# Regrouped wo rows and two reordered steps in a one-token attention and feed-forward kernel

## The chip, the cores and the metric

The kernel runs on 1 core of one Trainium2 chip. The metric is the device time of one execution in microseconds. Below, PE is TensorE, DVE is VectorE, ACT is ScalarE, and SP is the engine that issues nearly all DMAs here.

## What is computed

One token `x` (512 values, bf16) passes through attention over a cache of 65536 keys and values in 32 heads of 128, and beside it through a small feed-forward block; a scalar gate mixes the two.

```python
# H, Sk, Dh = 32, 65536, 128;  D = 512;  F = 1792
q = (x @ wq).reshape(H, Dh)
scores = einsum("hd,hkd->hk", q, k_cache) * Dh ** -0.5
o = einsum("hk,hkd->hd", softmax(scores), v_cache)
a = o.reshape(H * Dh) @ wo                    # wo: 4096 x 512
b = (silu(x @ w_gate) * (x @ w_up)) @ w_down
g = sigmoid((x * gate_w).sum())
out = g * a + (1 - g) * b
```

The two caches are 512 MB each, 1073.7 MB of the 1087.6 MB that are read. Keys and values are read once.

## The kernel before

**Tiling.** A head's 65536 keys are cut into 4 blocks of 128 x 128 keys; there are N = 128 blocks, numbered n = 4h + g, and M = 64 pairs of blocks, numbered i. A key block lies in SBUF as 128 partitions x 128 keys x 128 dimensions.

**Buffers.** Two slots take a pair of key blocks each (8 MB; `take` and `give`). `V_buf` takes a pair of value blocks; before that it holds wq, then w_gate, w_up and w_down. At the very end the two key slots are used again: `wo_early` holds wo of heads 0 to 15 and V block 124, `wo_late` holds V block 127 and wo of heads 16 to 31.

**Steps for a block n.** `products(n)` (DVE, L252 and L256) multiplies the keys with the broadcast q and halves the width by adding until 32 columns are left. `scores(n)` (PE, L265) adds these up with an identity as weights into PSUM; after it the key slot is free. `fold(n)` (DVE, L280) reduces the last four columns into `S_sb`. `values(n)` (PE, L321) multiplies the probabilities with the value block, 32 matmuls of 4 keys a partition each, into `O_ps`; after it that half of `V_buf` is free. For the very last block 30 matmuls do so, and 8 small ones (L339) the rest.

**Steps for a head h.** `query(h)` broadcasts q over the partitions (L166, L168, L170). `row_max(h)` and `exponentials(h)` find the maximum (a transpose on PE, L290) and make the probabilities (ACT, L299). `total(h)` adds the exponentials (PE, L307), `weight(h)` makes the factor gate / total, `rg` (DVE). `head_copy(h)` brings `O_ps` to SBUF (ACT, L331), `head_turn(h)` turns it into a column by 4 matmuls (L347) and writes that column, times `rg`, to `oT[:, h]` (ACT, L354). `project(h)` multiplies `oT[:, h]` with wo's 128 rows of head h into two accumulators (PE, L360).

**Loads.** `load_k`, `load_v` (L111) and `load_wo` (L176) are all issued from SP's queue in program order; each load waits there until its buffer is free, and what stands behind it waits as well. V blocks 125, 126 and 127 come in 2, 2 and 6 pieces (`V_CUTS`), wo's second half in 4 (`LATE_CUTS`). `load_wo` copies runs of one row of wo, 512 values, 1 KB: partition p gets row 128h + p for each head h.

**Order.** The order on each engine is that of the program, written out by hand; a loop over the 64 pairs interleaves the steps, so that values are two pairs behind the scores. In pair i PE does values(2i - 4), scores(2i) and values(2i - 3) and then scores(2i + 1); where a head starts (`first`), scores(2i) comes ahead of the values. w_down's product (`feed_forward_mid` on DVE, `feed_forward_out` on PE) comes in pair 1, after the first DVE step of products(3) and fold(2); behind it V block 0 is loaded, into the buffer that w_down leaves. In the last pair the projections of the first 16 heads stand ahead of scores(127). After the loop come head 31's softmax, head 30's turn, the last four values, head 31's turn and the projections of heads 16 to 31.

Of the kernel before, what the change touches and what calls it, by code (L numbers as in the profile page):

```python
# [8 lines left out]
ACT = mybir.ActivationFunctionType  # L9
ALU = mybir.AluOpType  # L10
AXIS = mybir.AxisListType
P = 128
# [7 lines left out]
QUAD = 4  # L20
# [3 lines left out]
TURNED = 8  # L24
V_CUTS = {3: (0, 64, NB), 2: (0, 64, NB), 1: (0, 32, 64, 96, 112, NB - TURNED, NB)}
EARLY = 16
LATE_CUTS = (EARLY, 21, 26, 30, 32)


@with_exitstack  # L30
def kernel(
# [14 lines left out]
    nc = tc.nc  # L46
# [11 lines left out]
    M = N // 2  # L58
    MH = G // 2
    assert Dh == P and G == 4 and NBH == 512 and H * D <= PAIR * Dh  # L60
    scale = float(Dh) ** -0.5
# [32 lines left out]
    with nc.allow_non_contiguous_dma(reason="small"):  # L94
# [4 lines left out]
        out=V_buf[:, : KT * H * Dh], in_=A_wq.rearrange("(p t) f -> p (t f)", t=KT)  # L99
# [3 lines left out]
    K_tiles, V_tiles, S_tiles, F_tiles, P_tiles, O_tiles, q_tiles = {}, {}, {}, {}, {}, {}, {}  # L103


    def load(view, cache, m, cuts, start=0):
        h, g = divmod(m, MH)
        rows = cache[0, h, g * PAIR * P : (g + 1) * PAIR * P, :]
        src = rows.rearrange("(p j) d -> p j d", j=PAIR)
        for a, b in zip(cuts[:-1], cuts[1:]):  # L110
            nc.sync.dma_start(out=view[:, a:b, :], in_=src[:, start + a : start + b, :])  # L111
# [7 lines left out]
    def load_v(n, half=0, spare=None):  # L119
        if n % G == 0 and spare is None:  # L120
            view = V_buf.rearrange("p (j d) -> p j d", d=Dh)
            V_tiles[n], V_tiles[n + 1] = view[:, :NB, :], view[:, NB:, :]
            load(view, A_v_cache, n // 2, (0, PAIR))
        else:
            view = V_buf if spare is None else spare
            view = view[:, half * NB * Dh : (half + 1) * NB * Dh]
            V_tiles[n] = view = view.rearrange("p (j d) -> p j d", d=Dh)
            load(view, A_v_cache, n // 2, V_CUTS.get(N - n, (0, NB)), n % 2 * NB)
# [16 lines left out]
    oT = consts.tile([P, H], bf16, name="oT")  # L145
    gval = consts.tile([P, 1], f32, name="gval")
    rg = consts.tile([P, H], f32, name="rg")
# [23 lines left out]

    def load_wo(tile, cuts):
        t = tile[:, : H * D].rearrange("p (h n) -> p h n", n=D)
        rows = A_wo.rearrange("(h p) n -> p h n", p=P)
        for a, b in zip(cuts[:-1], cuts[1:]):
            nc.sync.dma_start(out=t[:, a:b, :], in_=rows[:, a:b, :])  # L176
        return t

    def feed_forward_in():
# [63 lines left out]
    def width_of(n):  # L243
        return FIRST if n < G else WIDTH

    def products(n):
        K = K_tiles[n]
        qb = q_tiles[n // G][:, :]
        q_rep = bass.AP(
            tensor=qb.tensor, offset=qb.offset, ap=[list(qb.ap[0]), [0, NB], [1, Dh]]  # L250
        )
        yield nc.vector.tensor_tensor(out=K, in0=K, in1=q_rep, op=ALU.mult)  # L252
        half = Dh
        while half > width_of(n):
            half //= 2
            yield nc.vector.tensor_tensor(  # L256
                out=K[:, :, 0:half], in0=K[:, :, 0:half], in1=K[:, :, half : 2 * half],
                op=ALU.add,
            )

    def scores(n):
        S = F_tiles[n] = psum_s.tile([P, NB, QUAD], f32, name="S_ps")
        width = width_of(n)
        for c in range(0, width, QUAD):
            nc.tensor.matmul(  # L265
                S,
                lhsT=ident_b,
                rhs=K_tiles[n][:, :, c : c + QUAD],
                start=(c == 0),
                stop=(c == width - QUAD),  # L270
            )
        del K_tiles[n]
        if n % 2:
            give(f"K_t.{n // 2}")

    def fold(n):
        h, g = divmod(n, G)
        if g == 0:
            S_tiles[h] = small.tile([P, NBH], f32, name="S_sb")
        nc.vector.tensor_reduce(  # L280
            out=S_tiles[h][:, g * NB : (g + 1) * NB], in_=F_tiles.pop(n), axis=AXIS.X, op=ALU.add
        )
# [10 lines left out]
    def exponentials(h, mT_ps):  # L293
        top = small.tile([P, 1], f32, name="top")
        nc.vector.tensor_reduce(out=top, in_=mT_ps, axis=AXIS.X, op=ALU.max)  # L295
        bias = small.tile([P, 1], f32, name="bias")
        nc.scalar.activation(out=bias, in_=top, func=ACT.Copy, scale=-scale)  # L297
        P_tiles[h] = small.tile([P, NBH], bf16, name="P_sb")
        nc.scalar.activation(  # L299
            out=P_tiles[h], in_=S_tiles[h], func=ACT.Exp, bias=bias, scale=scale,  # L300
            accum_out=rowsum[:, h : h + 1],
        )
        del S_tiles[h]

    def total(h):
        tot_ps = psum_m.tile([P, 1], f32, name="tot_ps", tag="misc")
        nc.tensor.matmul(tot_ps, lhsT=ones_f, rhs=rowsum[:, h : h + 1], start=True, stop=True)  # L307
        return tot_ps
# [19 lines left out]

    def head_copy(h):
        O_sb = small.tile([4, 4 * Dh], f32, name="O_sb", tag="row", bufs=1)  # L330
        nc.scalar.activation(out=O_sb, in_=O_tiles.pop(h), func=ACT.Copy)  # L331
        return O_sb

    def head_turn(h, O_sb):
        oh_ps = psum_m.tile([P, 1], f32, name="oh_ps", tag="misc")
        turned = range(NB - TURNED, NB) if h == H - 1 else ()
        for j in turned:
            k = (G - 1) * NB + j
            nc.tensor.matmul(  # L339
                oh_ps,  # L340
                lhsT=V_tiles[N - 1][:, j, :],
                rhs=P_tiles[h][:, k : k + 1],
                start=(j == turned[0]),
                stop=False,
            )
        for c in range(4):
            nc.tensor.matmul(  # L347
                oh_ps,
                lhsT=O_sb[:, c * Dh : (c + 1) * Dh],
                rhs=ident_f[0:4, c : c + 1],  # L350
                start=(c == 0 and not turned),
                stop=(c == 3),
            )
        nc.scalar.activation(  # L354
            out=oT[:, h : h + 1], in_=oh_ps, func=ACT.Copy, scale=rg[:, h : h + 1]
        )

    def project(h):
        for i, a in enumerate(a_ps):
            nc.tensor.matmul(  # L360
                a,
                lhsT=oT[:, h : h + 1],
                rhs=wo_sb[:, h, i * HD : (i + 1) * HD],
                start=False,
                stop=(h == H - 1),
            )
# [11 lines left out]
    for i in range(M):  # L378
        h, first = i // MH, i % MH == 0
        vector = products(2 * i)  # L380
        next(vector)
        if mT_ps is not None:
            exponentials(h - 1, mT_ps)
        if not first:
            fold(2 * i - 1)
        for _ in vector:
            pass
        if first:
            scores(2 * i)
        if i >= 2:  # L390
            values(2 * i - 4)
            if first or i == M - 1:
                load_v(2 * i - 2 if first else N - 3)
        if not first:
            scores(2 * i)
        if i == 0:
            xs = gate_sum()
            eg2 = gate_exp(xs)
        if i >= 2:
            values(2 * i - 3)  # L400
            if first or i == M - 1:
                load_v(2 * i - 1 if first else N - 2, 1)
            else:
                load_v(2 * i - 2)
        if mT_ps is not None:
            tot_ps = total(h - 1)
            mT_ps = None
        if first and i > MH:
            head_turn(h - 2, head_copy(h - 2))
        vector = products(2 * i + 1)  # L410
        next(vector)
        fold(2 * i)
        if i == 1:
            hT = feed_forward_mid(*ff)
            feed_forward_out(hT, rest)
            load_v(0)
        for _ in vector:
            pass
        if i == 0:
            rest = gate_value(eg2)  # L420
        if tot_ps is not None:
            weight(h - 1, tot_ps)
            tot_ps = None
        if not first and h + 1 < H:
            query(h + 1)
        if i == M - 1:
            for o in range(EARLY):
                project(o)
        scores(2 * i + 1)
        if i == 0:  # L430
            ff = feed_forward_in()
        if i + 2 < M:
            load_k(i + 2)
        elif i + 2 == M:
            spare = take("wo_early.0")
            wo_sb = load_wo(spare, (0, EARLY))
            load_v(N - 4, 1, spare)
        if not first:
            fold(2 * i + 1)
            mT_ps = row_max(h)  # L440
    spare = take("wo_late.0")
    load_v(N - 1, 1, spare)
    exponentials(H - 1, mT_ps)
    tot_ps = total(H - 1)
    head_turn(H - 2, head_copy(H - 2))
    values(N - 4)
    values(N - 3)
    weight(H - 1, tot_ps)
    wo_sb = load_wo(spare, LATE_CUTS)
    values(N - 2)  # L450
# [39 lines left out]
```

## Time and profile before

| | |
|---|---|
| Median of 3 runs | 2529.11 us (2528.47 to 2530.81) |
| Profiled execution, its own time | 2529.75 us |
| Its span | 2528.0 us |
| Mean granted TensorE clock | 0.759 |
| Busy in the span: PE, DVE, ACT | 1415.6, 2065.9, 90.8 us |
| DMA | 1088.48 MB in 29577 packets, mean 431 GB/s |

The span is the time from the first to the last instruction of one profiled execution; its own time is the device time of that same execution. Busy times are sums over an engine's instructions. A row of the timeline gives start, duration, engine, line, operation and, in brackets, how long the engine was idle before it and what ended that. A row that merges several instructions has "xN" at its end. For SP's queue a merged row holds the time between the issues too. Matmul ends are modelled, so neighbouring PE rows can overlap by a fraction of a microsecond.

### The profile page before, as it was taken

Reading aid. Unit: us, or ns where it says so; the run is one execution under the profiler, and the core shown is the slowest. Engines: PE = TensorE matmul, PEld = TensorE weight load, DVE = VectorE, ACT = ScalarE, POOL = GpSimd, SP = SyncE. Lnnn points to the kernel's source line nnn. Section 1 sums busy time; section 2 is a strip of 40 time slices with the busy share of each in tenths; the row PEclk is TensorE's granted clock in tenths of the full one; section 3 lists DMA queues with packets and bytes.
Section 4 is the critical chain, followed back from the end, with each engine's and each line's share of the span. In section 5 each row is a group of like instructions: output and inputs, shape, how many; then the busy total and the mean of one; then the engine's idle time right before and its main releaser. Section 6 shows DMA issues by size and latency. Waiting matters only on the chain.

```text
span 2528.0 us, 13114 instructions
## 1 busy us (share of the span) xinstructions
PE 1415.6 (56%) x5898; PEld 548.2 (22%) x5898; DVE 2065.9 (82%) x648; ACT 90.8 (4%) x264; POOL 0.7 (0%) x6
## 2 busy tenths in 40 slices
PE   3655654646646456555465464665555655646648
PEld 2212221212212122222122121221212221212214
DVE  5897888887878878879888888788797888887882
ACT  0000000000000000000000000000000000000000
POOL 0000000000000000000000000000000000000000
PEclk9777777778777677777777776776867877768769
DMA  9999999999999999999999999999999999999998
GB/s 415 428 440 432 433 432 433 437 433 432 435 430 433 439 436 433 432 429 435 437 434 433 430 433 435 437 432 430 434 438 432 435 434 428 435 436 432 432 431 341
DMA packets 29577, 1088.48 MB, mean 431 GB/s; under 512 B 3153, under 2 KB 7250, under 8 KB 7634
## 3 DMA queue, kind: packets, MB, share of 16 engines
q1 hardware_dynamic: 29234, 1087.65, 99.6%
q8 instruction: 46, 0.75, 0.1%
q14 instruction: 9, 0.07, 0.0%
q10 hardware_dynamic: 288, 0.00, 0.0%
HBM read 1087.64 MB, written 0.00 MB: 430 GB/s over the span
## 4 chain that ended last, share of the span: by engine, by line
DMA 62%; PE 33%; DVE 4%; issue 0%; ACT 0%; another core or an unknown queue 0%; SPq 0%; DVEq 0%; ACTq 0%
DMA V_buf<-in_A_v_cache_dram 56%; PE O_ps L321 29%; DMA K_t<-in_A_k_cache_dram 6%; PE S_ps L265 3%; DVE K_t L252 3%; DVE K_t L256 1%; PE a_ps L360 0%; PE oh_ps L347 0%; PE b_ps L233 0%; DVE S_sb L280 0%; DVE top L295 0%; ACT O_sb L331 0%; PE a_ps L239 0%; PE qb_ps L168 0%
## 5 line engine op out<-in xcount | busy, mean ns | idle before, releaser
L252 DVE TENSOR_TENSOR K_t<-K_t,q_sb 128x16384 bf16<-128x16384 bf16 x128 | 1112.0, 8687 | 216.9 <-DMA K_t<-in_A_k_cache_dram 216.9
L321 PE MATMUL O_ps<-V_buf,P_sb 128*4 128x512 bf16 x4032 | 960.0, 401 | 363.0 <-DMA V_buf<-in_A_v_cache_dram 361.5
L256 DVE TENSOR_TENSOR K_t<-K_t 128x8192 bf16<-128x8192 bf16 x252 | 849.1, 3369 | 4.3
L265 PE MATMUL S_ps<-K_t,ident_b 128*128 128x512 bf16 x1056 | 352.9, 492 | 662.4 <-DVE K_t L256 662.4
L321 PEld LDWEIGHTS <-P_sb 128*4 128x4 bf16 x4094 | 359.3, 88 | 986.1 <-issue 524.2
L265 PEld LDWEIGHTS <-ident_b 128*128 128x128 bf16 x1056 | 116.1, 115 | 844.1 <-issue 759.6
L280 DVE TENSOR_REDUCE S_sb<-S_ps 128x128 f32<-128x512 f32 x128 | 87.6, 685 | 118.5 <-PE S_ps L265 118.5
L312 DVE RECIPROCAL recip<-tot_ps 128x1 f32<-128x1 f32 x32 | 5.4, 168 | 79.4 <-PE tot_ps L307 79.4
L290 PE MATMUL mT_ps<-diag,ones_f 128*128 128x128 f32 x64 | 21.5, 430 | 62.0 <-ACT diag L288 62.0
L170 ACT ACTIVATE q_sb<-qb_ps 128x128 bf16<-128x128 f32 x32 | 8.9, 277 | 955.2 <-PE qb_ps L168 955.2
L354 ACT ACTIVATE oT<-oh_ps,rg 128x1 bf16<-128x1 f32 x32 | 8.4, 264 | 736.6 <-PE oh_ps L347 736.6
L347 PE MATMUL oh_ps<-ident_f,O_sb 4*128 4x1 f32 x256 | 34.3, 251 | 0.5 <-ACT O_sb L331 0.5
L290 PEld LDWEIGHTS mT_ps<-diag,ones_f 128*128 128x128 f32 x64 | 13.4, 261 | 89.4 <-ACT diag L288 89.4
L347 PEld LDWEIGHTS oh_ps<-ident_f,O_sb 4*128 4x128 f32 x256 | 31.6, 190 | 1.2 <-ACT O_sb L331 0.7
L457 DVE CAST out_sb<-a_ps 1x256 bf16<-1x256 f32 x1 | 0.4, 411 | 36.6 <-PE a_ps L360 36.6
L288 ACT ACTIVATE diag<-ident_f,m 128x128 f32<-128x128 f32 x32 | 12.8, 401 | 303.0 <-DVE m L286 303.0
L299 ACT ACTIVATE P_sb<-S_sb,bias 128x512 bf16<-128x512 f32 x32 | 23.1, 722 | 1.0
L286 DVE TENSOR_REDUCE m<-S_sb 128x1 f32<-128x512 f32 x32 | 21.9, 686 | 1.1
L331 ACT ACTIVATE O_sb<-O_ps 4x512 f32<-4x512 f32 x32 | 18.2, 570 | 29.5 <-PE O_ps L321 29.5
L297 ACT ACTIVATE bias<-top 128x1 f32<-128x1 f32 x32 | 6.5, 203 | 327.2 <-DVE top L295 327.2
L307 PE MATMUL tot_ps<-rowsum,ones_f 128*128 128x1 f32 x64 | 12.2, 261 | 1.5 <-ACT P_sb L299 1.5
L307 PEld LDWEIGHTS tot_ps<-rowsum,ones_f 128*128 128x128 f32 x64 | 9.5, 188 | 15.2 <-issue 13.5
(48 smaller groups left out, 108.8 us busy)
## 6 DMA issues: line engine op xcount, KB each, us to landing
V_buf<-in_A_v_cache_dram SPq DMA_DIRECT2D x62, 4096.0 KB, 23.0
K_t<-in_A_k_cache_dram SPq DMA_DIRECT2D x4, 4096.0 KB, 32.5
V_buf<-in_A_v_cache_dram SPq DMA_DIRECT2D x4, 2048.0 KB, 25.0
V_buf<-in_A_wq_dram SPq DMA_DIRECT2D x1, 4096.0 KB, 12.5
wo_early<-in_A_v_cache_dram SPq DMA_DIRECT2D x1, 4096.0 KB, 35.4
wo_late<-in_A_v_cache_dram SPq DMA_DIRECT2D x3, 1024.0 KB, 25.1
wo_early<-in_A_wo_dram SPq DMA_DIRECT2D x1, 2048.0 KB
V_buf<-in_B_w_gate_dram SPq DMA_DIRECT2D x1, 1792.0 KB, 54.6
```

The costliest lines, as they stand in the source:

```text
L252: yield nc.vector.tensor_tensor(out=K, in0=K, in1=q_rep, op=ALU.mult)
L256: yield nc.vector.tensor_tensor(out=K[:, :, 0:half], in0=K[:, :, 0:half], in1=K[:, :, half : 2 * half], op=ALU.add,)
L265: nc.tensor.matmul(S, lhsT=ident_b, rhs=K_tiles[n][:, :, c : c + QUAD], start=(c == 0), stop=(c == width - QUAD),)
L280: nc.vector.tensor_reduce(out=S_tiles[h][:, g * NB : (g + 1) * NB], in_=F_tiles.pop(n), axis=AXIS.X, op=ALU.add)
L286: nc.vector.tensor_reduce(out=m, in_=S_tiles[h], axis=AXIS.X, op=ALU.max)
L288: nc.scalar.activation(out=diag, in_=ident_f, func=ACT.Copy, scale=m)
L290: nc.tensor.matmul(mT_ps, lhsT=ones_f, rhs=diag, start=True, stop=True)
L299: nc.scalar.activation(out=P_tiles[h], in_=S_tiles[h], func=ACT.Exp, bias=bias, scale=scale, accum_out=rowsum[:, h : h + 1],)
L307: nc.tensor.matmul(tot_ps, lhsT=ones_f, rhs=rowsum[:, h : h + 1], start=True, stop=True)
L321: nc.tensor.matmul(O_tiles[h], lhsT=P_tiles[h][:, g * NB + j : g * NB + j + 4], rhs=V_tiles[n][:, j : j + 4, :], start=(g == 0 and j == 0) ...
L331: nc.scalar.activation(out=O_sb, in_=O_tiles.pop(h), func=ACT.Copy)
L347: nc.tensor.matmul(oh_ps, lhsT=O_sb[:, c * Dh : (c + 1) * Dh], rhs=ident_f[0:4, c : c + 1], start=(c == 0 and not turned), stop=(c == 3),)
```

## The change

`load_wo` reads wo in groups of four heads: of the 512 rows of a group, partition p now gets rows 4p to 4p + 3, one run of 4 KB. This holds for heads 0 to 27; the pieces of the last four heads stay as they were, and the late pieces are cut at 24, 28 and 30 instead of 21, 26 and 30. So that the projections still match, the column of `oT` for group member j has to hold, in partition p, the group's output 4p + j. `head_copy` therefore copies `O_ps` in another order of its columns, and `head_turn` writes a head's column in four strips of 32 partitions to four columns of `oT`: four ACT copies in place of one.

Three steps move. In the last pair scores(126) goes ahead of values(122). In pair 1 w_down's product, and the load of V block 0 behind it, go ahead of products(3) and fold(2). The projections of the first 16 heads go from ahead of scores(127) to behind the exponentials of the last head, ahead of its total.

```diff
-LATE_CUTS = (EARLY, 21, 26, 30, 32)
+LATE_CUTS = (EARLY, 24, 28, 30, 32)
+GROUPED = 28
...
     def load_wo(tile, cuts):
         t = tile[:, : H * D].rearrange("p (h n) -> p h n", n=D)
+        runs = t.rearrange("p (g j) n -> p g (j n)", j=QUAD)
         rows = A_wo.rearrange("(h p) n -> p h n", p=P)
+        row_runs = A_wo.rearrange("(g p j) n -> p g (j n)", p=P, j=QUAD)
         for a, b in zip(cuts[:-1], cuts[1:]):
-            nc.sync.dma_start(out=t[:, a:b, :], in_=rows[:, a:b, :])
+            if b <= GROUPED:
+                a, b = a // QUAD, b // QUAD
+                nc.sync.dma_start(out=runs[:, a:b, :], in_=row_runs[:, a:b, :])
+            else:
+                nc.sync.dma_start(out=t[:, a:b, :], in_=rows[:, a:b, :])
         return t
...
     def head_copy(h):
         O_sb = small.tile([4, 4 * Dh], f32, name="O_sb", tag="row", bufs=1)
-        nc.scalar.activation(out=O_sb, in_=O_tiles.pop(h), func=ACT.Copy)
+        src, dst = O_tiles.pop(h)[:, :], O_sb[:, :]
+        if h < GROUPED:
+            src = src.rearrange("q (c a j) -> q c j a", c=4, j=QUAD)
+            dst = dst.rearrange("q (c j a) -> q c j a", c=4, j=QUAD)
+        nc.scalar.activation(out=dst, in_=src, func=ACT.Copy)
         return O_sb
...
-        nc.scalar.activation(
-            out=oT[:, h : h + 1], in_=oh_ps, func=ACT.Copy, scale=rg[:, h : h + 1]
-        )
+        if h >= GROUPED:
+            nc.scalar.activation(
+                out=oT[:, h : h + 1], in_=oh_ps, func=ACT.Copy, scale=rg[:, h : h + 1]
+            )
+            return
+        g, part = divmod(h, QUAD)
+        A = P // QUAD
+        for j in range(QUAD):
+            nc.scalar.activation(
+                out=oT[part * A : (part + 1) * A, g * QUAD + j : g * QUAD + j + 1],
+                in_=oh_ps[j * A : (j + 1) * A, :],
+                func=ACT.Copy,
+                scale=rg[j * A : (j + 1) * A, h : h + 1],
+            )
...
-        if first:
+        if first or i == M - 1:
             scores(2 * i)
         if i >= 2:
             values(2 * i - 4)
             if first or i == M - 1:
                 load_v(2 * i - 2 if first else N - 3)
-        if not first:
+        if not first and i < M - 1:
             scores(2 * i)
...
-        vector = products(2 * i + 1)
-        next(vector)
-        fold(2 * i)
         if i == 1:
             hT = feed_forward_mid(*ff)
             feed_forward_out(hT, rest)
             load_v(0)
+        vector = products(2 * i + 1)
+        next(vector)
+        fold(2 * i)
         for _ in vector:
             pass
...
-        if i == M - 1:
-            for o in range(EARLY):
-                project(o)
         scores(2 * i + 1)
...
     exponentials(H - 1, mT_ps)
+    for o in range(EARLY):
+        project(o)
     tot_ps = total(H - 1)
```

## The prediction

> **What bounds the kernel now.** I read the page first: span, queues and groups of instructions.
>
> ```profile
> span 2528.0 us, 13114 instructions
> ...
> DMA packets 29577, 1088.48 MB, mean 431 GB/s; under 512 B 3153, under 2 KB 7250, under 8 KB 7634
> ...
> q1 hardware_dynamic: 29234, 1087.65, 99.6%
> ...
> L354 ACT ACTIVATE oT<-oh_ps,rg 128x1 bf16<-128x1 f32 x32 | 8.4, 264 | 736.6 <-PE oh_ps L347 736.6
> ...
> L331 ACT ACTIVATE O_sb<-O_ps 4x512 f32<-4x512 f32 x32 | 18.2, 570 | 29.5 <-PE O_ps L321 29.5
> ```
>
> SP's queue keeps the sixteen DMA engines full: 99.6% of the span goes into 1087.65 MB. The 4097 packets between 512 B and 2 KB (7250 less 3153) are wo: 4096 rows of 1 KB, and one more. Then the busy times by stretch.
>
> ```profile
> 100.00:2400.00 2300.00, 1290.43 (x5170) 490.59 (x5170) 1926.21 (x595) 78.94 (x232) 0.00 (x0) 0.75 1.00 434
> 2467.00:2473.00 6.00, 6.00 (x28) 2.21 (x27) 6.00 (x3) 0.00 (x0) 0.00 (x0) 1.00 0.76 260
> 2511.00:2516.00 5.00, 5.00 (x25) 1.96 (x23) 0.00 (x0) 0.00 (x0) 0.00 (x0) 1.00 1.06 393
> 2520.10:2528.00 7.90, 4.90 (x48) 3.75 (x48) 0.41 (x1) 1.22 (x3) 0.00 (x0) 1.00 0.01 3
> ```
>
> The last three columns are the granted TensorE clock, the DMA share and GB/s. From 100 to 2400 us the DMA share is 1.00 at 434 GB/s: whatever an engine gains there waits for the next transfer. Only in the last 70 us is it otherwise: a dip to 260 GB/s at 2467 to 2473, and after 2520 no transfer at all while PE still works. So I read that end instruction by instruction, PE's timeline first.
>
> ```profile
> 2461.32 8.64 PE L321 MATMUL O_ps<-V_buf,P_sb 128*4 128x512 bf16 x32 [11.28 <-DMA V_buf<-in_A_v_cache_dram]
> 2469.89 1.90 PE L265 MATMUL S_ps<-K_t,ident_b 128*128 128x512 bf16 x8
> 2471.73 7.07 PE L321 MATMUL O_ps<-V_buf,P_sb 128*4 128x512 bf16 x32
> 2478.63 3.66 PE L360 MATMUL a_ps<-wo_early,oT 128*1 128x256 bf16 x32
> 2482.22 1.90 PE L265 MATMUL S_ps<-K_t,ident_b 128*128 128x512 bf16 x8
> 2486.06 0.49 PE L290 MATMUL mT_ps<-diag,ones_f 128*128 128x128 f32 x2 [1.94 <-ACT diag L288]
> 2488.01 0.38 PE L307 MATMUL tot_ps<-rowsum,ones_f 128*128 128x1 f32 x2 [1.46 <-ACT P_sb L299]
> 2488.49 1.86 PE L347 MATMUL oh_ps<-ident_f,O_sb 4*128 4x1 f32 x8
> 2490.28 9.52 PE L321 MATMUL O_ps<-wo_early,P_sb 128*4 128x512 bf16 x32
> 2499.63 13.98 PE L321 MATMUL O_ps<-V_buf,P_sb 128*4 128x512 bf16 x64
> 2513.45 6.64 PE L321 MATMUL O_ps<-wo_late,P_sb 128*4 128x512 bf16 x30
> 2520.02 0.35 PE L339 MATMUL oh_ps<-P_sb,wo_late 128*128 128x1 bf16 x8
> 2520.82 1.05 PE L347 MATMUL oh_ps<-ident_f,O_sb 4*128 4x1 f32 x8 [0.45 <-ACT O_sb L331]
> 2521.80 3.65 PE L360 MATMUL a_ps<-wo_late,oT 128*1 128x256 bf16 x32
> ```
>
> In order these are values(122), scores(126), values(123), the sixteen early projects, scores(127), the transpose of the last maximum, its total, head 30's turn, values(124) to values(127), the last head's turn and the late projects. From 2461.32 on PE waits 1.94, 1.46 and 0.45 us and never for a transfer. PE sets the end, and the question is what the new order does to it.
>
> **The end, part by part.** Two moves matter. Scores(126) goes ahead of values(122), and the early projects go from before scores(127) to behind the transpose of the maximum. DVE feeds both scores:
>
> ```profile
> 2456.74 6.74 DVE L256 TENSOR_TENSOR K_t<-K_t 128x8192 bf16<-128x8192 bf16 x2
> ...
> 2472.61 6.74 DVE L256 TENSOR_TENSOR K_t<-K_t 128x8192 bf16<-128x8192 bf16 x2
> ```
>
> Products(126) are ready at 2456.74 + 6.74 = 2463.48, products(127) at 2479.35. So scores(126), now first, holds values(122) from 2461.32 until 2463.5 and then its own length. Behind the wait on PE stand values(122), values(123), scores(127); behind those on SP's queue the loads of V 125, 126 and 127 into the halves that they free.
>
> First stretch, until the end of scores(127). PE comes from 11 us of idleness, so it starts at half clock; values(122) paid 8.64 - 7.07 = 1.6 for that, values(124) paid 9.52 - 7.0 = 2.5 (7.0 is half of 13.98). I take 2.2 for the later start. After: 2463.5 + 1.90 + 7.07 + 7.07 + 1.90 + 2.2 = 2483.6. DVE's 2479.35 is earlier and does not hold it. Before it was 2482.22 + 1.90 = 2484.1. Gain 0.5, between 0.2 and 1.1 with the two penalties: 3.6 us of projects leave this stretch, but PE's work in it can begin only at 2463.5, 2.2 us after V 122 has landed, and pays more at half clock.
>
> Second stretch, from there to values(124): before, 2490.28 - 2484.12 = 6.16. After: wait 1.94, transpose 0.49, projects 3.59 (2478.63 to 2482.22), total 0.48, head 30's turn 1.05 at full clock (the last head's row) = 7.55. The projects fill the 1.46 us wait for the exponentials, but stick out by 2.1; at full clock the turn gives 0.8 back. Loss 1.4. Values(124) starts at 2491.2 instead of 2490.3: 0.9 later.
>
> Third stretch, the clock. Here are the windows of 3.4 us that the changes of the granted clock mark.
>
> ```profile
> 2485.00:2488.40 3.40, 0.87 (x4) 0.59 (x4) 0.86 (x2) 1.85 (x5) 0.00 (x0) 1.00 0.99 424
> 2488.40:2491.80 3.40, 3.31 (x12) 2.24 (x13) 0.33 (x2) 0.30 (x2) 0.00 (x0) 0.51 1.02 439
> 2491.80:2495.20 3.40, 3.40 (x9) 1.02 (x8) 0.00 (x0) 0.00 (x0) 0.00 (x0) 0.50 0.99 419
> ```
>
> PE was busy 0.87 of 3.4 us, and for the next two windows the clock was 0.5. That made values(124) last 9.35 to its successor instead of 7.0. After, the only gap is 1.94 us, with work without a break behind it, so a window holds at least 1.4 us of work. I take it that the clock stays: values(124) gains 2.36. Values(125) then starts 0.9 - 2.36 = 1.45 us earlier, and all behind it as well, because the rest keeps its order and its lengths.
>
> The Trainium skill, "TensorE: Matmul & The Clock Gate", Part 1 (the table of states), lets the clock fall only after at least one idle window of about 3.4 us. The trace differs: the window of 2485.0 was a quarter busy and the clock fell. By the page alone the kernel before would have had no slow stretch here, values(124) would have nothing to win, and the sum would be 0.9 slower; the measurement decides.
>
> **wo in groups.** 28 of 32 heads come as 896 runs of 4 KB instead of 3584 of 1 KB; the last four stay. At 1 KB the engines carry 393 / 1.06 = 371 GB/s in a full share against 434, so 2.1 MB take 5.65 instead of 4.83 us: 0.8 for the early half, 0.6 for 12 of the 16 late heads. The dip at 2467 loses (434 - 260) x 6 / 434 = 2.4 us more. Whom does it help? SP's queue:
>
> ```profile
> 2450.50 20.47 SPq L111 DMA_DIRECT2D wo_early<-in_A_v_cache_dram  x1
> 2471.06 8.09 SPq L111 DMA_DIRECT2D V_buf<-in_A_v_cache_dram  x4
> 2484.16 12.24 SPq L111 DMA_DIRECT2D wo_late<-in_A_v_cache_dram  x6
> ```
>
> and, from the DMA issues, the us from issue to landing at the end of the row:
>
> ```profile
> wo_early<-in_A_v_cache_dram SPq DMA_DIRECT2D x1, 4096.0 KB, 35.4
> ...
> wo_late<-in_A_v_cache_dram SPq DMA_DIRECT2D x3, 1024.0 KB, 25.1
> ```
>
> The issue of V 124 stood 20.47 us behind wo's 2048 descriptors; that will go. But V 124 landed at 2450.50 + 35.4 = 2485.9, 4.4 us before its use at 2490.28, and V 127's first three megabytes landed near 2484.5 + 25.1 = 2509.6 in the middle, where PE asks for the second at 2513.45 + 1.75 = 2515.2. wo had landed by about 2520 (3 GB/s from 2520.1 on); its use begins at 2521.80. So PE waits for none of it and I book zero; the cover is 4.4 us for V 124, 5.6 for V 127 and 1.7 for wo, and PE asks 1.45 earlier, while the transfers gain at least the 0.8 and 0.6 above. The load of V 125 moves from 2471.06 by at most 3.4 us, still 11 us before V 124 has landed, so the queue does not run dry: zero as well.
>
> **The start.** Feed_forward_mid and w_down's product go ahead of products(3).
>
> ```profile
> 76.87 5.72 PE L233 MATMUL b_ps<-V_buf,hT 128*1 128x512 bf16 x14 [3.95 <-DVE hT L227]
> ```
>
> ```profile
> 56.64 0.33 SPq L111 DMA_DIRECT2D K_t<-in_A_k_cache_dram  x1
> 82.62 0.33 SPq L111 DMA_DIRECT2D V_buf<-in_A_v_cache_dram  x1
> ```
>
> ```profile
> K_t<-in_A_k_cache_dram SPq DMA_DIRECT2D x1, 28.7
> ```
>
> PE waited 3.95 us for hT; without that V 0 is issued at about 78.7 instead of 82.6. K's load issued at 56.64 was in flight until 85.3, so the queue had work in both cases: zero. DVE gets 0.9 us of small work earlier instead of later: zero.
>
> **Per head, 28 times.** Three more ACT copies, 3 x 0.264 = 0.8 us, and O_sb's copy in a strided order (0.57 us; the trace shows no strided one, so 0.3 to 1.1, and I take 0.57). Queued behind them is only the next head's diagonal, whose product's copy comes 30 us later:
>
> ```profile
> 2370.22 0.39 ACT L166 ACTIVATE q_diag<-ident_f,qT 128x128 bf16<-128x128 f32 x1
> 2400.69 0.28 ACT L170 ACTIVATE q_sb<-qb_ps 128x128 bf16<-128x128 f32 x1 [30.08 <-PE qb_ps L168]
> ```
>
> Zero, with 30 us of cover. None of heads 28 to 31, which are copied at the end, is changed.
>
> **Sum.** 2529.75 (this execution; the span and 1.75 around it) - 1.45 = 2528.3. The median of the runs, 2529.11, is 0.64 lower, so 2527.7. 0.2% is 5.1 us, about what a measurement of this kernel can tell from no change: the forecast is inside.
>
> **Rivals.** A, transfers set the end. The 2.4 of the dip and the 0.8 and 0.6 of the packets then come on top of PE's 1.45: 5.25, that is 2523.9. For it: the dip, and the DMA share of 1.06 at a low rate. Against: not one wait of PE on a transfer after 2461.32. It decides if V 124 to 127 are used within a microsecond of landing. 0.12.
>
> B, the clock falls in the 1.94 us gap all the same. A window with 0.43 of work lies between what the trace shows to let it fall (0.26) and what surely holds it. The projects and the turn then run slowly or values(124) does: half of one or two windows, 1.7 to 3.4, and I take 2.4; the sum becomes + 1.0, so 2530.1. 0.16.
>
> C, slower: the strips are on the chain. If the ACT queue of each head (its 0.8 us) delays what frees a V buffer or makes the next q, 28 x 0.8 = 22 us appear, 2551. Its place is oT's copies behind each turn; it decides only if they outlast the 30 us of cover. ACT is busy 78.94 of 2300 us. 0.06.
>
> **Numbers.** Forecast 0.66 and B 0.16 are both within 0.2%: same 0.82; A faster 0.12; C slower 0.06. The forecast's own terms (0.2 to 1.1, a penalty of 1.6 to 2.5) and the runs' spread (2528.47 to 2530.81) make 2525.8 to 2529.8; B's upper side reaches 2531.0, and the dip's 2.4 alone, taken from 2527.7, gives 2525.3. Range 2525.0 to 2531.0, which leaves out A and C, 0.18.
>
> **What will show it.** Scores(126) before values(122), which starts near 2467; scores(127) ends near 2483.6; PE's one gap of 1.9 before the transpose and the projects right behind it; values(124) at about 2491 lasting 7.0 at clock 1.00; no dip at 2467 and no issue of 20 us; packets between 512 B and 2 KB down from 4097 to 513. Wrong I would be if PE waits for V or wo after 2461, if the clock is 0.5 after 2488, or if the rate between 100 and 2400 us is not 434.

## The result and the profile after

The changed kernel takes 2525.95 us (median of 19 runs, 2525.11 to 2527.31); the kernel before, in as many runs beside it, 2530.24 us (2528.47 to 2531.40). The ratio is 0.9984, with a 95% interval of 0.9978 to 0.9991: 4.3 us or 0.17% faster, a small change that is clear of zero. The profiled execution took 2525.51 us, 4.24 less than the profiled one of before. The forecast gain was 1.45 us, a third of that. The direction was forecast and the time lies in the range, but the size was not forecast: 2.8 us came from places that had been booked at zero or too small.

First, from the page of the changed kernel, the packets and the strips that replace the single copies of `oT`. Lines in the changed file are shifted: scores are L273, values L329, projections L385, the transpose L298, the total L315, the turn L359, products L260 and L264.

```profile
DMA packets 26890, 1088.49 MB, mean 431 GB/s; under 512 B 3153, under 2 KB 3666, under 8 KB 4946
...
L376 ACT ACTIVATE oT<-oh_ps,rg 32x1 bf16<-32x1 f32 x112 | 28.6, 255 | 683.5 <-PE oh_ps L359 682.4
```

The packets between 512 B and 2 KB are 513 (3666 less 3153) instead of 4097, and there are 112 strips, four for each of 28 heads: the change does what it says. Now PE's timeline of the end, against the fourteen rows of the prediction.

```profile
2461.89 3.57 PE L273 MATMUL S_ps<-K_t,ident_b 128*128 128x512 bf16 x8 [13.50 <-DVE K_t L264]
2465.39 14.03 PE L329 MATMUL O_ps<-V_buf,P_sb 128*4 128x512 bf16 x64
2479.35 1.90 PE L273 MATMUL S_ps<-K_t,ident_b 128*128 128x512 bf16 x8
2483.20 0.49 PE L298 MATMUL mT_ps<-diag,ones_f 128*128 128x128 f32 x2 [1.94 <-ACT diag L296]
2483.61 3.65 PE L385 MATMUL a_ps<-wo_early,oT 128*1 128x256 bf16 x32
2487.20 0.38 PE L315 MATMUL tot_ps<-rowsum,ones_f 128*128 128x1 f32 x2
2487.51 1.05 PE L359 MATMUL oh_ps<-ident_f,O_sb 4*128 4x1 f32 x8
2488.49 7.07 PE L329 MATMUL O_ps<-wo_early,P_sb 128*4 128x512 bf16 x32
2495.39 13.98 PE L329 MATMUL O_ps<-V_buf,P_sb 128*4 128x512 bf16 x64
...
2517.56 3.65 PE L385 MATMUL a_ps<-wo_late,oT 128*1 128x256 bf16 x32
```

Scores(126) now waits for products(126). Of the two gaps before values(124) only the one of 1.94 us is left, the projections run right behind the transpose, and values(124) takes 6.90 us to its successor instead of 9.35. No row here waits for a transfer. What the prediction did not have is seen one step earlier, on DVE: the start of products(126), first in the kernel before, then in the changed kernel.

```profile
2447.54 8.68 DVE L252 TENSOR_TENSOR K_t<-K_t,q_sb 128x16384 bf16<-128x16384 bf16 x1
```

```profile
2445.89 8.68 DVE L260 TENSOR_TENSOR K_t<-K_t,q_sb 128x16384 bf16<-128x16384 bf16 x1
```

The last stretch begins 1.65 us earlier. That splits the 4.24 us between the two profiled executions (times in us; the first row is a time, the others are lengths):

| Stretch | before | after | difference | forecast |
|---|---|---|---|---|
| until products(126) starts | 2447.54 | 2445.89 | -1.65 | 0 |
| from there to the end of scores(127) | 36.58 | 35.36 | -1.22 | -0.5 |
| to the start of values(124) | 6.16 | 7.24 | +1.08 | +1.4 |
| values(124) | 9.35 | 6.90 | -2.45 | -2.36 |
| to the late projections | 22.17 | 22.17 | 0 | 0 |

And wo itself: the issue of V 124 behind it in the queue, and the stretch that had been a dip.

```profile
2448.86 0.50 SPq L113 DMA_DIRECT2D wo_early<-in_A_v_cache_dram  x1
```

```profile
2467.00:2473.00 6.00, 6.00 (x30) 2.34 (x28) 6.00 (x3) 0.00 (x0) 0.00 (x0) 1.00 0.98 414
```

The issue takes 0.50 us instead of 20.47, and in place of the dip to 260 GB/s stand 414. The time alone does not tell whether either is worth anything.

### The profile page after: what moved, and what is told of

Its sections match the earlier page's. It is cut to its first block, busy times and chain, and to the rows that moved or that the text cites. A ratio compares the mean times of both kernels' runs of the same rounds, so it can differ in the third digit from the quotient of the medians.

```text
span 2523.7 us, 13226 instructions
## 1 busy us (share of the span) xinstructions
PE 1411.6 (56%) x5898; PEld 547.1 (22%) x5898; DVE 2066.2 (82%) x648; ACT 115.2 (5%) x348; POOL 0.7 (0%) x6
## 2 busy tenths in 40 slices
DMA packets 26890, 1088.49 MB, mean 431 GB/s; under 512 B 3153, under 2 KB 3666, under 8 KB 4946
## 4 chain that ended last, share of the span: by engine, by line
DMA 62%; PE 33%; DVE 5%; issue 0%; another core or an unknown queue 0%; ACT 0%; SPq 0%; DVEq 0%; ACTq 0%
DMA V_buf<-in_A_v_cache_dram 58%; PE O_ps L329 29%; DMA K_t<-in_A_k_cache_dram 4%; PE S_ps L273 3%; DVE K_t L260 3%; DVE K_t L264 2%; PE a_ps L385 0%; PE oh_ps L359 0%; DVE S_sb L288 0%; PE tot_ps L315 0%; PE qb_ps L170 0%; DVE m L294 0%; DVE top L303 0%; ACT O_sb L343 0%
## 5 line engine op out<-in xcount | busy, mean ns | idle before, releaser
L260 DVE TENSOR_TENSOR K_t<-K_t,q_sb 128x16384 bf16<-128x16384 bf16 x128 | 1112.1, 8688 | 216.8 <-DMA K_t<-in_A_k_cache_dram 216.8
L329 PE MATMUL O_ps<-V_buf,P_sb 128*4 128x512 bf16 x4032 | 955.9, 400 | 356.3 <-DMA V_buf<-in_A_v_cache_dram 354.9
L264 DVE TENSOR_TENSOR K_t<-K_t 128x8192 bf16<-128x8192 bf16 x252 | 849.3, 3370 | 4.3
L273 PE MATMUL S_ps<-K_t,ident_b 128*128 128x512 bf16 x1056 | 358.6, 499 | 674.9 <-DVE K_t L264 674.9
L329 PEld LDWEIGHTS <-P_sb 128*4 128x4 bf16 x4094 | 358.0, 88 | 973.6 <-issue 507.9
L273 PEld LDWEIGHTS <-ident_b 128*128 128x128 bf16 x1056 | 117.7, 116 | 861.3 <-issue 783.4
L376 ACT ACTIVATE oT<-oh_ps,rg 32x1 bf16<-32x1 f32 x112 | 28.6, 255 | 683.5 <-PE oh_ps L359 682.4
L298 PE MATMUL mT_ps<-diag,ones_f 128*128 128x128 f32 x64 | 21.5, 430 | 62.0 <-ACT diag L296 62.0
L359 PE MATMUL oh_ps<-ident_f,O_sb 4*128 4x1 f32 x256 | 33.5, 248 | 0.5 <-ACT O_sb L343 0.5
L298 PEld LDWEIGHTS mT_ps<-diag,ones_f 128*128 128x128 f32 x64 | 13.4, 262 | 89.8 <-ACT diag L296 89.8
L359 PEld LDWEIGHTS oh_ps<-ident_f,O_sb 4*128 4x128 f32 x256 | 30.8, 186 | 1.0 <-ACT O_sb L343 0.5
L168 ACT ACTIVATE q_diag<-ident_f,qT 128x128 bf16<-128x128 f32 x32 | 12.8, 400 | 0.4
L315 PEld LDWEIGHTS tot_ps<-rowsum,ones_f 128*128 128x128 f32 x64 | 9.5, 188 | 13.8 <-issue 13.8
```

The costliest lines, as they stand in the source:

```text
L168: nc.scalar.activation(out=diag, in_=ident_f, func=ACT.Copy, scale=qT[:, h : h + 1])
L264: yield nc.vector.tensor_tensor(out=K[:, :, 0:half], in0=K[:, :, 0:half], in1=K[:, :, half : 2 * half], op=ALU.add,)
L273: nc.tensor.matmul(S, lhsT=ident_b, rhs=K_tiles[n][:, :, c : c + QUAD], start=(c == 0), stop=(c == width - QUAD),)
L298: nc.tensor.matmul(mT_ps, lhsT=ones_f, rhs=diag, start=True, stop=True)
L329: nc.tensor.matmul(O_tiles[h], lhsT=P_tiles[h][:, g * NB + j : g * NB + j + 4], rhs=V_tiles[n][:, j : j + 4, :], start=(g == 0 and j == 0) ...
L359: nc.tensor.matmul(oh_ps, lhsT=O_sb[:, c * Dh : (c + 1) * Dh], rhs=ident_f[0:4, c : c + 1], start=(c == 0 and not turned), stop=(c == 3),)
```

## The experiments

The change has four parts: wo in groups, and three moved steps (the title counts two). Each run below is timed against the kernel before, beside it on the same chip; differences are between the two medians, of 11 executions of each variant and 15 to 33 of the kernel before.

### The start alone

```diff
-        vector = products(2 * i + 1)
-        next(vector)
-        fold(2 * i)
         if i == 1:
             hT = feed_forward_mid(*ff)
             feed_forward_out(hT, rest)
             load_v(0)
+        vector = products(2 * i + 1)
+        next(vector)
+        fold(2 * i)
```

> The kernel before, with nothing but w_down's product and V block 0's load moved ahead of products(3). Theory T (the DMA engines ran dry at 84 to 86 us, since V 0 was issued only 2.7 us ahead of the landing of the last piece of K in flight): V 0 is issued near 76.5 instead of 82.6, no second without transfers at 85, later K and V blocks land 0.9 to 1.4 us earlier through the whole kernel, median 1.0 to 1.6 us below before. Rival R (a load in flight is cover enough, as predicted): V 0 lands no earlier, median within 0.4 us of before, and the 1.6 us by which the changed kernel's end began earlier came from elsewhere.

2528.57 us against 2529.70, ratio 0.9997 (0.9989 to 1.0006): 1.1 faster in the medians, though the interval does not exclude no change. The traces are plainer. Here are the issue of V 0 with the earlier start, then the stretch from 84 to 86 us, first before and then with the earlier start, which is followed by one row more; the last column is GB/s.

```profile
76.14 0.33 SPq L111 DMA_DIRECT2D V_buf<-in_A_v_cache_dram  x1
```

```profile
84.00:86.00 2.00, 2.00 (x11) 0.84 (x10) 0.00 (x0) 0.28 (x1) 0.00 (x0) 1.00 0.24 98
```

```profile
84.00:86.00 2.00, 2.00 (x7) 0.71 (x6) 0.00 (x0) 0.00 (x0) 0.00 (x0) 0.60 1.21 524
86.00:88.00 2.00, 0.99 (x5) 0.25 (x3) 0.94 (x2) 0.00 (x0) 0.00 (x0) 1.00 0.30 131
```

Such short rows have to be read with care. They count a packet wholly where it starts, and a packet of these loads has 64 KB and takes 2.42 us in the trace, longer than a row. So the 98 GB/s do not mean idle engines, and with the earlier start a low row of 131 merely stands elsewhere. With the bytes spread over each packet's own duration, the kernel before lost 0.93 us of transfers at 434 GB/s between 82 and 94 us. About 0.2 of that is engines without a packet, around 83.6. The rest is the first packets of V 0, most of which took 3.0 to 3.5 us instead of 2.42. With V 0 issued at 76.14 instead of 82.62, 0.00 us are lost.

Products(12), the start of a head that waits for its keys, comes 1.14 us earlier. From 125 us to the end the key loads of this one execution are issued 0.0 to 2.0 us earlier than before, 0.9 in the mean. The five profiles with the old start (the kernel before, and the runs below of wo, the projections, scores(126) and the clock alone) bear it out: in the order of their losses, 0.11, 0.28, 0.62, 0.93 and 1.15 us, they start products(126) at 2446.18, 2446.76, 2447.14, 2447.54 and 2447.82. In all eight profiles with the earlier start the loss is 0.00, and products(126) start between 2445.80 and 2446.97.

### The start later

```diff
+        for _ in vector:
+            pass
         if i == 1:
             hT = feed_forward_mid(*ff)
             feed_forward_out(hT, rest)
             load_v(0)
-        for _ in vector:
-            pass
```

> The kernel before, with w_down's product and V block 0's load moved the other way: behind all of products(3). V 0 is then issued near 87.8 instead of 82.6. Theory T (the engines run dry before the last piece of K lands, and the first bytes of V come some 2 us after the issue, so each us of later issue beyond about 81.5 costs one): no transfers for about 5 us around 87, every later load 4.5 to 5.5 us later, 4.5 to 5.5 us slower. Rival R (dry only from the landing of K at 85.3 to the issue): 2 to 3 us slower. If the earlier start's 1.1 us had nothing to do with the queue: within 0.5 us of before.

2534.20 us against 2529.82, ratio 1.0018 (1.0009 to 1.0027): 4.4 slower. Here are the queue's issues of K and V 0, the time from issue to landing of K, and three stretches of 2 us:

```profile
57.20 0.33 SPq L111 DMA_DIRECT2D K_t<-in_A_k_cache_dram  x1
87.07 0.33 SPq L111 DMA_DIRECT2D V_buf<-in_A_v_cache_dram  x1
```

```profile
K_t<-in_A_k_cache_dram SPq DMA_DIRECT2D x1, 28.2
```

```profile
82.00:84.00 2.00, 2.00 (x6) 0.64 (x5) 0.00 (x0) 0.00 (x0) 0.00 (x0) 0.50 0.16 66
84.00:86.00 2.00, 2.00 (x6) 0.64 (x5) 0.00 (x0) 0.00 (x0) 0.00 (x0) 0.50 0.00 0
86.00:88.00 2.00, 1.23 (x5) 0.21 (x3) 0.00 (x0) 0.92 (x2) 0.00 (x0) 0.85 0.00 0
```

K counts as landed at 57.20 + 28.2 = 85.4, but only two of the large packets start after 82, and none between 84 and 88. By their starts and durations, 14 of 16 engines end their last packet of K by 83.6, about 2 us before the landing is reported, and the other two at 85.0. The first packets of V 0 start at 88.04, about 1 us behind the issue. In all 5.32 us of transfers are lost between 82 and 94 us, 4.4 more than before, and the kernel became 4.4 us longer. V 0 was issued 4.45 us later than before: in this range each microsecond of issue costs one. That is the theory's case; "dry from landing to issue" would have given 2 to 3. (The 4.5 to 5.5 expected were for an issue at 87.8; it came at 87.07.)

### wo in groups alone

The three moves are undone; the layout, the reordered copies and the strips stay.

> The changed wo layout with its reordered copies and strips, and the order of the steps as before. Theory T (PE's chain sets the end, wo is covered): V 124's issue no longer stands 20 us, the dip at 2467 goes, packets of 1 KB are 513, and the time stays within 0.5 us of before. Rival R (transfers carry part of it): 1.5 to 3.8 us faster, by the dip's 2.4 and the packets' 1.4 us. If the strips of 28 heads cost anything on the chain it is slower by up to 22 us.

2529.79 against 2529.70, ratio 1.0000 (0.9992 to 1.0009). The dip is gone here as well:

```profile
2467.00:2473.00 6.00, 6.00 (x28) 2.26 (x26) 4.31 (x1) 0.00 (x0) 0.00 (x0) 0.99 1.02 431
```

By the rates, 2.4 us of transfers are won in that stretch, and none of them shows in the time: they were covered. That speaks against rival A for the kernel before. The strips of 28 heads cost nothing that can be measured, so rival C, with its 22 us, is out.

### The projections alone

```diff
-        if i == M - 1:
-            for o in range(EARLY):
-                project(o)
         scores(2 * i + 1)
 ...
     exponentials(H - 1, mT_ps)
+    for o in range(EARLY):
+        project(o)
```

> The kernel before, with nothing but the early projections moved behind the exponentials. Theory T (PE's chain, clock included): scores(127) starts when products(127) are ready, 2479.4 instead of 2482.2 (-2.85); total and turn come 1.1 later by the projections that stick out; the clock stays at 1.0, so that values(124) takes 6.9 to 7.0 instead of 9.35 (-2.4): 4.2 us faster. Rival R (transfers): values(124) to (127) or the late projections then wait for V or for wo in 1 KB rows, and 2 us or less remain. Second rival (the clock falls in the 1.94 us gap as well): 1.8 us faster.

2526.55 against 2529.70, ratio 0.9987 (0.9978 to 0.9996): 3.15 faster, between the theory's 4.2 and the rivals' 2 or less. PE's timeline says where most of the missing microsecond is.

```profile
2479.68 1.89 PE L265 MATMUL S_ps<-K_t,ident_b 128*128 128x512 bf16 x8 [0.66 <-DVE K_t L256]
...
2488.80 7.07 PE L321 MATMUL O_ps<-wo_early,P_sb 128*4 128x512 bf16 x32
...
2518.07 2.34 PE L360 MATMUL a_ps<-wo_late,oT 128*1 128x256 bf16 x20
2520.78 1.47 PE L360 MATMUL a_ps<-wo_late,oT 128*1 128x256 bf16 x12 [0.36 <-DMA wo_late<-in_A_wo_dram]
```

Scores(127) starts when DVE allows, and values(124) keeps the full clock, both as expected (-2.8 and -2.45, with +1.1 in between). But the late projections wait for wo: from their first to their last it is 4.2 us instead of 3.65. That is half of the missing microsecond. Values(127) takes 0.2 longer than the 6.64 of before, and 0.3 lies in the start, since products(126) begin at 2447.82 in this execution. So once PE is more than 3 us earlier, 1 KB rows cost half a microsecond.

### Scores(126) alone

```diff
-        if first:
+        if first or i == M - 1:
             scores(2 * i)
 ...
-        if not first:
+        if not first and i < M - 1:
             scores(2 * i)
```

> The kernel before, with nothing but scores(126) moved ahead of values(122). Theory T: PE idles until products(126) are ready at 2463.5, so that values(122) starts at 2467 instead of 2461.3 and scores(127), still behind values(123) and the projections, ends 2.0 to 2.5 us later; everything behind it follows, the clock falls as before: 2.0 to 2.5 us slower. Rival R (the move is what made the changed kernel's end earlier): 1 us or more faster.

2531.48 against 2529.70, ratio 1.0009 (1.0000 to 1.0017): 1.8 slower. The move makes PE wait:

```profile
2463.14 3.57 PE L265 MATMUL S_ps<-K_t,ident_b 128*128 128x512 bf16 x8 [13.50 <-DVE K_t L256]
...
2484.04 1.90 PE L265 MATMUL S_ps<-K_t,ident_b 128*128 128x512 bf16 x8
```

13.50 us of idleness, ended by DVE, where before 11.28 were ended by V 122's landing. Scores(127) ends 38.8 us after the start of products(126) (2447.14 here) instead of 36.6: 2.2 later, as expected, and everything behind follows; the medians, at 1.8, are a little below the 2.0 to 2.5 expected. So this move works against the change, and the projections' move outweighs it.

### The clock alone

```diff
         scores(2 * i + 1)
+        if i == M - 1:
+            pad(8, h - 1)
 ...
     exponentials(H - 1, mT_ps)
+    pad(6, H - 2)
     tot_ps = total(H - 1)
```

> The kernel before, with 14 matmuls added whose results nobody reads: 8 of 128x512 behind scores(127) and 6 ahead of the last total, in PE's gaps of 1.94 and 1.46 us (8 x 0.219 = 1.75 and 6 x 0.219 = 1.31, so they fit). Nothing else moves. Theory T (the clock falls because of these gaps, and that is what the late projections cure): clock 1.0 throughout, head 30's turn 1.05 instead of 1.4 to 1.9, values(124) 7.0 instead of 9.4 to 10.0: 2.4 to 3.5 us faster, at the price of no earlier step. Rival R (a gap shorter than one whole window of 3.4 us does not let the clock fall; values(124) is slow for another cause, V 124's late landing say): within 0.5 us of before.

2527.23 against 2529.75, ratio 0.9990 (0.9981 to 0.9998): 2.5 faster, with fourteen useless matmuls more (`pad` writes 128x512 into a tile that nobody reads) and no step earlier. PE's timeline, and the granted clock (third column from the end) of the window with the transpose and of the next:

```profile
2484.17 1.89 PE L361 MATMUL pad_ps<-P_sb,ident_b 128*128 128x512 bf16 x8
...
2488.70 1.05 PE L347 MATMUL oh_ps<-ident_f,O_sb 4*128 4x1 f32 x8
2489.68 7.07 PE L321 MATMUL O_ps<-wo_early,P_sb 128*4 128x512 bf16 x32
```

```profile
2484.40:2487.80 3.40, 3.19 (x16) 1.38 (x14) 1.64 (x3) 1.05 (x3) 0.00 (x0) 1.00 1.01 434
2487.80:2491.20 3.40, 3.14 (x20) 1.87 (x19) 0.33 (x2) 1.11 (x4) 0.00 (x0) 1.00 0.97 414
```

The clock stays at 1.00 and values(124) takes 6.90 to its successor: the third stretch of the table comes from PE's idleness, and V 124's landing has no part in it. The rows would give 3.3 us (2.45 in values(124), 0.8 in head 30's turn); why the medians show 0.7 less is open.

### The changed kernel without scores(126) in front

> The changed kernel with scores(126) put back behind values(122). Theory T (PE's chain; that move costs): values(122) starts at V 122's landing, near 2460.5, scores(127) when products(127) are ready, near 2478 to 2479 instead of 2479.35: 0.5 to 1.3 us faster than the changed kernel, 4.8 to 5.6 faster than before. Rival R (the move helps): 1 us slower than the changed kernel, 3.3 faster than before.

2525.08 against 2529.75, ratio 0.9983 (0.9974 to 0.9991): 4.7 faster, just under the 4.8 to 5.6 expected. PE's rows first, then DVE's fold(126), in the changed kernel and here:

```profile
2460.61 9.14 PE L329 MATMUL O_ps<-V_buf,P_sb 128*4 128x512 bf16 x32 [12.04 <-DMA V_buf<-in_A_v_cache_dram]
...
2479.02 1.89 PE L273 MATMUL S_ps<-K_t,ident_b 128*128 128x512 bf16 x8 [0.44 <-DVE K_t L264]
```

```profile
2470.36 0.68 DVE L288 TENSOR_REDUCE S_sb<-S_ps 128x128 f32<-128x512 f32 x1
```

```profile
2471.62 0.69 DVE L288 TENSOR_REDUCE S_sb<-S_ps 128x128 f32<-128x512 f32 x1 [1.01 <-PE S_ps L273]
```

Values(122) starts at V 122's landing again, and scores(127) at 2479.02 instead of 2479.35. Less is won than was lost in the run of that move alone (1.8), because another engine now holds scores(127). In the changed kernel it is PE: scores(127) follows values(123) without a gap, and products(127) are ready before, at 2477.7. Here it is DVE: fold(126), which stands inside products(127), waits 1.01 us for scores(126), now behind values(122) at half clock.

### The projections cut in two, with wo in groups and without

```diff
         scores(2 * i + 1)
+        if i == M - 1:
+            for o in range(EARLY // 2):
+                project(o)
 ...
     exponentials(H - 1, mT_ps)
-    for o in range(EARLY):
+    for o in range(EARLY // 2, EARLY):
         project(o)
```

> As the run before it in this call, and the sixteen early projections cut in two: eight behind scores(127), in the gap of 1.94 us (8 x 0.229 = 1.83), eight behind the last transpose, in the gap of 1.46 us. Theory T (PE's chain): total and turn come 1.4 to 1.8 us earlier: 6.2 to 7.2 us faster than before. Rival R (transfers): values(124) would start near 2486, V 127's second megabyte be asked for at 2508.5 and the last wo at 2518.5, within 0.5 us of their landings; then PE waits for V or wo and the gain stops near 5.5.

> The earlier start of V block 0 and the projections cut in two as in the run before it, but wo in rows of 1 KB as before. Theory T (the regrouped wo is worth nothing as long as PE is late, and something once PE is early): PE waits for late wo pieces, and perhaps for V 127, by 1 to 2.5 us, so 4 to 5.5 us faster than before, 1 to 2.5 less than with wo in groups. Rival R (PE's chain alone, wo covered): as fast as with wo in groups, within 0.4.

Both have the earlier start and leave scores(126) behind values(122), as the run above; they differ in wo alone.

2524.60 with groups, 0.9980 (0.9971 to 0.9989), and 2525.11 with rows of 1 KB, 0.9982 (0.9973 to 0.9991), both against 2529.75: 5.2 and 4.6 faster. With groups first, then without:

```profile
2486.19 7.07 PE L329 MATMUL O_ps<-wo_early,P_sb 128*4 128x512 bf16 x32
2493.10 10.52 PE L329 MATMUL O_ps<-V_buf,P_sb 128*4 128x512 bf16 x48
2504.26 3.61 PE L329 MATMUL O_ps<-V_buf,P_sb 128*4 128x512 bf16 x16 [0.64 <-DMA V_buf<-in_A_v_cache_dram]
2507.71 3.62 PE L329 MATMUL O_ps<-wo_late,P_sb 128*4 128x512 bf16 x16
2511.59 3.18 PE L329 MATMUL O_ps<-wo_late,P_sb 128*4 128x512 bf16 x14 [0.26 <-DMA wo_late<-in_A_v_cache_dram]
```

```profile
2504.68 3.61 PE L321 MATMUL O_ps<-V_buf,P_sb 128*4 128x512 bf16 x16 [1.16 <-DMA V_buf<-in_A_v_cache_dram]
```

Values(124) starts at 2486.2, 2.3 us earlier than in the changed kernel, but PE now waits for the second half of V 126 and for V 127. That is rival A's case at last: the PE chain lost its lead, and the gain stops at 5.2 instead of 6.2 to 7.2. Here the grouped wo is worth half a microsecond, less than the 1 to 2.5 expected: without it V 126 lets PE go 0.42 us later (2504.68 against 2504.26), and the rest is in the late projections. Why no more of the dip's 2.4 us shows is open.

### Three versions side by side

> The changed kernel once more, for a comparison on one chip with the next two. Theory: 4.2 to 4.4 us faster than before, as measured.

> The changed kernel with scores(126) put back behind values(122), beside the changed kernel on the same chip. Theory T (the move costs PE the wait for products(126)): 0.3 to 1.0 us faster than the changed kernel. Rival R (nothing, the medians of two calls differed by chance): within 0.2 us of it.

> The same with the early projections cut in two, beside the changed kernel on the same chip. Theory T (PE 2 us earlier, then held by V 126, V 127 and wo): 0.9 to 1.6 us faster than the changed kernel. Rival R (transfers hold the changed kernel already): within 0.4 us of it.

On one chip against 2529.47: the changed kernel 2525.98 (0.9986, 0.9977 to 0.9994; 2525.01 to 2528.59), without scores(126) in front 2525.37 (0.9982, 0.9974 to 0.9991), with the projections cut as well 2524.63 (0.9980, 0.9971 to 0.9989; 2524.45 to 2524.86). The changed kernel is 3.5 faster than before here, less than the 4.2 to 4.4 expected. The 0.6 and 1.35 us between the three lie in what was expected, but the intervals against before overlap, so the order rests on medians of 11 runs each. The longest run of the changed kernel, 2528.59, is the profiled one, and it shows something more:

```profile
2481.70:2485.10 3.40, 1.46 (x8) 0.59 (x7) 1.38 (x2) 0.40 (x1) 0.00 (x0) 1.00 0.92 395
2485.10:2488.50 3.40, 3.40 (x18) 1.99 (x17) 0.29 (x1) 1.49 (x4) 0.00 (x0) 0.51 1.02 439
```

```profile
2485.01 5.32 PE L385 MATMUL a_ps<-wo_early,oT 128*1 128x256 bf16 x32
```

In this execution a clock window lay so that it held the whole gap of 1.94 us and 1.46 us of work, and the clock fell: the projections took 5.32 us instead of 3.65. That is rival B, seen in one of the two profiles of the changed kernel. With the projections cut in two there is no gap at the transpose, and the runs spread over 0.4 us instead of 3.6 (on the other chip ten of eleven within 0.3, and one at 2526.30). That the clock is what spreads the unprofiled runs is not shown.

## Why the prediction was right, and where it was not

**Right: what sets the end.** PE's chain from 2461 on does, and not wo, as wo alone (0.1 us) and the padded gaps (2.5) show. The third stretch was forecast at -2.36 and measured at -2.45; the second at +1.4 and +1.08, since the rows of the transpose, the total and the turn overlap their neighbours a little.

**Right: the strips, and zero for wo.** Both hold as long as PE is no more than about 3 us earlier. The cover was given as 4.4, 5.6 and 1.7 us. The 5.6 is too large: it took one landing for the middle of three, and by the trace V 127's second megabyte landed at 2510.6, 4.6 us before PE asks for it, and the third 3.9 before. V 126 was not given; its second half had 4.4. With the projections alone moved, 3 us earlier, PE waited 0.36 us for 1 KB wo rows, and 2.3 us beyond the changed kernel it waited for V 126.

**Wrong: "K's load issued at 56.64 was in flight until 85.3, so the queue had work in both cases: zero."** That step is the main error. A load in flight does not keep all engines at work until its landing is reported: with V 0 issued late, 14 of 16 had no packet from 83.6 on, while K landed at 85.4. Before, V 0 was issued at 82.62, and 0.93 us of transfers were lost behind it. They are not made up, because the next 2300 us run at the rate of transfers (a DMA share of 1.00). Measured: -1.1 in the median for the start alone, +4.4 with V 0 4.45 us later; lost transfers, by the traces: 0.93 us less and 4.4 more. So about 1 of the profiled 1.65 us is explained. The rest is within what executions differ by: in the eight profiles with the earlier start products(126) begin anywhere between 2445.80 and 2446.97. The prediction was also off in the issue itself, which it put at 78.7; it came at 76.52.

**Too small: the first stretch,** -0.5 for -1.22. The step is its penalty at half clock: 2.2 us were added to 1.90 for scores(126), and the row has 3.57 in all, a penalty of 1.7, with the values at nearly full clock behind it. In the longest run side by side, the values behind it took 15.15 us instead of 14.03, so these two profiles give 1.7 and 2.8. PE had started at 2461.9 and 2462.2, and the clock came back at 2465.5 in the one and at 2468.1 in the other. The prediction saw, but did not follow up, that scores(126) in front is what costs here: its own sum shows PE starting 2.2 us later, and left behind the values the medians are 0.6 us lower on one chip.

**Luck.** The measured 2525.95 lies in the stated range of 2525.0 to 2531.0 by less than 1 us. The forecast's own terms and the spread of the runs reached down to 2525.8; the range went lower only for the dip's 2.4 us, which wo alone shows to be worth nothing here. What took the time there instead was above all the start, which had been booked at zero.

**The Trainium skill's rule on the clock,** "TensorE: Matmul & The Clock Gate", Part 1: the clock falls after at least one idle window. The trace had one case against it (0.87 of 3.40 us busy and it fell); the longest run side by side adds 1.46 of 3.40. In the changed kernel's first profile windows with 2.06 and more kept the clock. By the rule as it stands the changed kernel's clock would not have fallen; in one of its two profiles it did.

## What to carry to other kernels

Where a long stretch runs at the rate of transfers, look at what comes before it: a load that was issued 2.7 us before the previous one landed had already cost 0.9 us here, and what was lost there was not won back. Read the rate in short windows only with the length of a packet in mind. In a tail that one engine sets, put work into its gaps instead of behind them, in pieces that fit, both for the time and for the clock. Small descriptors, a dip in the rate and a blocked issue cost what the reader of that data waits, which here was nothing until the reader was 3 us earlier.

## What the runs showed of the hardware that was not expected

Of 16 engines 14 had their last packet of K behind them about 2 us before its landing was reported, and the first packets of V 0, issued late or as before, started about 1 us behind the issue; most of them took 2.7 to 3.6 us instead of 2.42, and why they are slower is open. A packet of 1 KB took 46 ns, one of 4 KB 159 ns and one of 64 KB 2.42 us, which for sixteen engines is 356, 412 and 434 GB/s; the prediction's 371 for 1 KB was read from a stretch that also held larger packets. The clock fell after a window that was 43% busy (1.46 of 3.40 us), and stayed after one of 61% (2.06 of 3.40), in the changed kernel's first profile:

```profile
2479.20:2482.60 3.40, 2.06 (x10) 0.69 (x8) 1.27 (x2) 0.00 (x0) 0.00 (x0) 1.00 0.94 405
```

An issue of 4 MB stood 20.47 us in SP's queue behind 2048 runs of 1 KB, and 0.50 us behind 512 runs of 4 KB, without a measurable difference in the kernel's time.
